# A new order of issue: gates' and down products in longer runs on TensorE

## The chip, the cores and the metric

One core of a Trainium2 chip runs the whole program. The metric is the device time of one execution in microseconds (us), and the time of a kernel is the median of several executions. Engines are named as in the profile: PE is TensorE (PEld its weight loads), DVE VectorE, ACT ScalarE, POOL GpSimd, and SP SyncE, which here only issues DMAs.

## The reference

An attention over 8 batches, 8 heads, 576 positions and 64 channels feeds a gated product chain over the 4608 tokens:

```python
q_d, k_d, v_d = (means of q, k, v over 4 positions)
out_up = repeat(softmax(q_d @ k_d.T / 8) @ v_d, 4)
mask = abs(pos[:, None] - pos[None, :]) < 4
out_local = softmax(where(mask, q @ k.T / 8, -1e9)) @ v
x = (out_up + out_local), as 4608 tokens x 512
a = x @ w1                      # 512 -> 1024
b = x @ w2
h = a * b @ w3                  # 1024 -> 1024
return h @ w_out                # 1024 -> 512
```

The inputs q, k, v and the four weights arrive as float32 or float64; the kernel takes the weights as 64-bit words where they are that.

## The kernel before, in words

**Stages.** First the product of `w3` and `w_out` is formed (`fold`, tasks `product m j`), so that `h @ w_out` becomes one product with 1024 rows and 512 columns, kept as a high and a low half in `wphl`. The weights come from HBM as 64-bit words in tiles `raw`, and DVE and ACT make float32 and then a high and a low part of each (`words`, `parted`, `gate_block`). Beside this runs the attention: `pooled` and `quad` for the part on means of four positions, and for the local part either `group_unit` with its scores and values on PE (the first two batches) or `unit` on DVE and ACT (the other six), where DVE multiplies and adds tiles of 128 x 768. Each unit ends in x, again a high and a low part, `xh` and `xl`.

**The chain of products.** The tokens go through `moe(c)` in 12 chunks of 384. For each chunk and each eighth `f` of the 1024 columns there are two gates' products, `which` 0 for `w1` and 1 for `w2`, into one PSUM tile `pab` each, 128 x 384. Each is two tasks of 6 matmuls. `three` (L317 to L319) issues the three matmuls of one product of high and low parts. Then ACT copies the first tile out (`copy_a`, L1062), DVE multiplies it with the second tile (L1064), ACT rounds the result to its high part `gh` (L1069) and DVE takes the low part `gl` (L1071). A down product of chunk c and eighth f is three tasks of three matmuls, `wphl` times `gh` and `gl`, summed over f in three PSUM tiles `acc`. There are two `pab` tiles (`BUFS["ab"]`), three `acc` tiles and three for everything else (`s_ps`, `t_ps`, `o_ps`, `se_ps`, `te_ps`, `oe_ps`). In the first gates' weights of a chunk (f 0 to 3) `w1a` belongs to the first tile and `w2a` to the second; for later f both are in `wo` or both in `wb`.

**What sets the order.** Nothing is scheduled on the chip. `Plan.add` collects 3208 tasks with their dependences and buffers (`Ring`). The table `ORDER` says, engine by engine, in which order that engine's tasks are issued; a number in it is the place of a task among its engine's tasks as `Plan.add` saw them, "78-86" a row of them. `Plan.order` merges the five lists, and each engine then runs its own list strictly in order, with waits where a task needs another's result or buffer:

```python
left[e] = [l[k] for w in ORDER[e].split() for a, _, b in [w.partition("-")]
           for k in range(int(a), int(b or a) + 1)][::-1]
```

A `pab` tile's next user is thus bound to its last reader by the ring of two:

```python
t, bank = add("PE", 6 * mm_us(CT), mmul, d, take=[R["ab"]], uses=[x_held[c]])
ta, ha = add("ACT", act_us(CT, psum=True), copy_a, [ends[0]], take=[R["a"]], uses=[banks[0]])
tg = add("DVE", dve_us(CT), ..., [ta, ends[1]], uses=[ha, banks[1]])
```

In the first 100 us SP's list also decides which load comes first: of the words of the weights (`raw`, L342), of `q` and `k` for `pooled_sums` (L688, L692) and of the values `v_w` for `group_unit` (L732).

Of the kernel before, what the change touches and what calls it, by code (L numbers as in the profile page):

```python
# [64 lines left out]
        "31-34 37 35-36 38-43 45 44 48 47 46 50-51 49 53 52 55-56 54 59 58 57 2 61 60 3 64 63 62 5 67 66 4 65 68-69 71-72 70 73 79 78 81 "  # L65
        "76 6 80 74-75 82 84 83 0 7 87 86 85 89 88 8 11 9-10 13 12 77 91-92 95 90 94 14-16 93 1 96-97 104 107 17 103 18-19 106 105 20 98 "
        "21-22 108-109 111 23 112 110 25-26 114 28 27 24 115 117 113 116 29 119 30 99-100 122 120 118 102 145 123 128 101 125 121 124 "
        "146 126 147 131 167 166 127 173 130 133 174-175 168 149 129 148 172 132 134 170-171 164-165 169 151 150 135-136 188 137 189-190 "
        "138 191 184 152 178 183 153 139-141 176 181 143 177 142 179 187 144 194 182 195 197 196 186 192 201 198 200 199 193 180 202-203 "
        "155 154 185 204 208 206 205 209 207 156 215 212 214 213 211 210 157 218 217 216 158 219-222 224 223 225 159 257 226 253 248 256 "  # L70
        "252 250 247 160 251 255 254 249 246 264 269 260 259 267 261 270 265 262 258 271 273 272 263 227 266 268 161-162 274 276 279 277 "
        "275 278 229 280 228 281 230-231 163 302-303 305 304 308 306 233 331 307 309 232 329 334 330 235 332-333 310 337-338 335-336 340 "
        "339 341 234 312-313 315 237 342 301 348 343 236 344-345 349 346 238 347 316-317 350 311 358 355 239 357 351 356 359 314 352 240 "
        "353 360 366 241 323 320 364 363 365 322 361-362 321 282 319 318 367 242 368-370 326 371-372 243 324 373 325 244 405 400 374 "
        "283-284 403 327 245 401-402 404 409 285 375-377 286 328 378 408 379 427 406 430 428 288 429 407 410 287 289 411 431-432 354 412 "
        "290 433-434 413 435-436 454 457 292 291 414 459 415 458 416 419 460 455-456 465 417 437 293-294 418 420 380 421 441 422 442 423 "
        "461-462 295-296 463 424 440 439 438 464 466 445 297 447-448 381 443 446 444 467-468 382 469-470 298 471 449 383 499 472 451 299 "
        "450 426 473 300 474-475 384 502 476 504 385 477 506 501 478 503 507 500 509 387 508 386 452 510 571 389 505 425 572-573 388 "
        "511-512 574 513 391 577 575 578 390 514-515 518-519 516 453 576 520 517 521-522 393 523 529 479 579 392 530 526-527 534 532 525 "
        "395 528 535 531 533 394 581 584 582 585 536 396 480 580 583 586 537 591 538-539 397 587 590 398 540 482 541-542 598 603 544 481 "  # L80
        "543 545 399 484 546-548 483 588 592 599 601 605 589 607 549 485 608-609 486 600 602 488 604 487 606 570 594 593 595 610 489 596 "
        "611-612 490 613 524 614 625 617-618 615-616 629 619 627 624 491 620 550 492 634 621 493 628 622 635 626 632 696 494-495 630 698 "
        "697 631 633 699 636 551-552 637 703 638 496 701 700 702 597 553 639-640 643 641-642 497 669 554-555 704 644-645 670 646 498 "
        "647-648 671-672 706 557 709 673-674 710 677 556 675 711 678 559 679-680 558 708 707 676 714 681 561 682 623 560 683-684 688 685 "
        "689 563 686-687 725 690 712 562 691 649 565 713 692-693 564 734 728 727 733 705 723 715 717 724 726 732 566 695 650 716 730-731 "
        "729 735 651-652 720 736-737 719 738 718 739 771 740 567 654 741 769 772 653 742 568 721 743 722 744 773 569 745 768 770 746 774 "
        "778 656 747 779 775 655 776 840-843 777 658 780 844 657 781-782 694 660 847 794 846 795 659 799 783 787 784 661 785-786 662 845 "
        "663 788-789 797 748 790-792 801 664 798 796 803 665 805 800 804 848 749 802 806 666 750 807-808 751 809-811 850 667-668 852 851 "
        "872 854 853 867 813 753 855 812 814-815 752 877 754 816 870 868 755 871 859 869 817 878 818 849 757 861 860 874 856 873 858 857 "
        "839 756 876 875 793 863 758 879 759 880-882 761 883 864 862 894 884 886-887 897 888 885 865 819 889 760 896 895 890-891 763 893 "  # L90
        "965 901 898 904 968 966 902 967 866 900 762 899 820 764 903 905 765 906 969 907 821 970 822 908-909 766 971-972 941 823 910 767 "
        "911 824 938 912 939 943 942 940 825-826 913-914 973 915-917 945 827 944 828 948 946-947 949 892 950 830 995 829 996 951 997 994 "
        "832 975 952 957 953 992 831 958 954-955 833 956 993 918 978 976 959-960 834 1002 835 980 919 961 1000 998 962 977 1003 979 985 "
        "999 920-921 1001 836 981 1004-1005 837 1006-1007 923 838 1008-1010 983 922 1037 1040 1039 925 1041-1042 1011-1013 924 974 986 "
        "1038 927 1014-1015 1043 1016 1045 926 1048 982 1044 984 963 929 1046 989 928 987-988 1047 930 964 1049 1064 931 990-991 1050 "
        "1068 1066 932 1067 1051 1017 1056-1057 933 1052 1063 1053 1058 1054-1055 934 1059 1074 1072-1073 1018 1065 1071 935 1069 "
        "1019-1020 1060 936 1061 937 1021-1022 1070 1075-1076 1023 1077-1078 1024 1079-1081 1026 1082-1085 1025 1086-1087 1028 1062 1027 "
        "1030 1029 1031 1088 1032-1033 1089 1034 1091 1035 1090 1092-1093 1036 1095 1094 1097 1096 1099 1098 1101 1100 1102-1106"
    ),
    DVE=(  # L100
        "1 0 55 2 56 3 57 59-61 4 58 62 5-7 63 8 11-12 9-10 64 13-14 66-67 15 65 69 22 68 71 73 70 74 23 72 76 32 31 75 33 78 80 77 81 "
        "79 16 83 82 85 87 34 84 86 35 88 38 36 90 37 89 91 17 96 98 94 99 97 92-93 100 40 18 101 39 103 102 41 19-20 105 104 24 42 106 "
        "43 46 45 44 108 107 110 112 25 30 109 21 26 111 27 113 119 181 121 95 120 114 123 28-29 47 124 48-49 122 182 130 183 125-126 50 "
        "128 131 51 127 52-53 129 54 115 173 116 133 180 132 137 135 174 157 117 138 175 136 176 134 159 158 139-140 142 118 144 187 184 "
        "145 141 146 191 143 161 188 177 160 192 178-179 194-195 163 162 185 147 196 189 148-149 197 190 193 150 186 151 201 152 154-155 "
# [1138 lines left out]
```

## Time and profile before

| what | value |
|---|---|
| median of 3 executions | 752.03 us (750.47 to 754.09) |
| the profiled execution, its own time | 751.62 us |
| its span, first to last instruction | 749.8 us |
| PE busy | 734.5 us, 98% of the span, 5378 matmuls |
| DVE busy | 612.3 us, 82% |
| ACT busy | 534.9 us, 71% |
| POOL busy | 110.9 us, 15% |
| mean granted clock of PE | 0.997 of full speed |

The profile is one execution. Busy time is what an engine's instructions covered; on PE matmuls overlap, and their ends are modelled, so the time from one start to the next tells more than the duration. In a timeline a row has the start in us from the span's begin, the duration in us, the engine, the line, the operation, what it writes and reads, and in brackets the idle time before it and what ended that.

### The profile page before, as it was taken

What the parts mean: (1) busy time and instruction counts of PE and PEld (TensorE: products, weight loads), DVE (VectorE), ACT (ScalarE), POOL (GpSimd) and SP (SyncE); (2) the same over time, 40 slices, a digit from 0 to 9 for tenths busy, and PEclk for the clock granted to TensorE, in tenths of its full rate; (3) what the DMA queues carried; (4) which work ended last, traced back from release to release, by engine and by line L of the source; (5) the groups of instructions that cost most, each with busy time, mean ns of one, the idle gap of its engine ahead of it and who ended that gap; (6) DMA issues with size and microseconds to landing.
All of it is one profiled execution on the core that took longest, in us unless ns stands there. A gap on an engine that the chain in (4) does not pass through costs nothing.

```text
span 749.8 us, 14982 instructions
## 1 busy us (share of the span) xinstructions
PE 734.5 (98%) x5378; PEld 661.8 (88%) x5378; DVE 612.3 (82%) x1028; ACT 534.9 (71%) x2101; POOL 110.9 (15%) x147
## 2 busy tenths in 40 slices
PE   7998999999999999999999999999999999999996
PEld 6776888888999989999989989899899999999995
DVE  5998996448999998999999999898999898865112
ACT  4897878567997976986886986787687795742211
POOL 4020003300212211122111211131120010010000
PEclk9999999999999999999999999999999999999999
DMA  9898855724786767498367764488555345322101
GB/s 306 268 278 253 270 163 110 139 56 143 176 219 153 167 154 208 97 209 218 66 168 195 155 160 128 109 206 208 141 95 151 98 95 149 83 46 41 43 1 42
DMA packets 49887, 111.91 MB, mean 149 GB/s; under 512 B 4996, under 2 KB 17284, under 8 KB 49812
## 3 DMA queue, kind: packets, MB, share of 16 engines
q0 software_dynamic: 14592, 38.94, 29.8%
q1 hardware_dynamic: 34932, 71.74, 28.8%
q8 instruction: 42, 0.69, 0.4%
q10 hardware_dynamic: 288, 0.27, 0.1%
q14 instruction: 33, 0.27, 0.1%
HBM read 80.26 MB, written 9.44 MB: 120 GB/s over the span
## 4 chain that ended last, share of the span: by engine, by line
PE 77%; DVE 11%; DMA 4%; ACT 4%; issue 2%; SPq 0%; DVEq 0%; ACTq 0%
PE pab L317 16%; PE pab L319 16%; PE pab L318 16%; PE acc L317 8%; PE acc L318 8%; PE acc L319 8%; DMA raw<-in_w_dram 3%; PE s_ps L614 2%; PE o_ps L575 1%; DVE wx L364 1%; PE t_ps L656 1%; ACT junk L911 1%; DMA xl<-pv 1%; DVE pr L901 1%; PE oe_ps L829 1%
## 5 line engine op out<-in xcount | busy, mean ns | idle before, releaser
L959 ACT ACTIVATE pv<-kv,s 128x64 f32<-128x64 f32 x432 | 116.9, 338 | 16.2 <-DVE s L936 14.7
L911 ACT ACTIVATE junk<-pr 128x64 f32<-128x64 f32 x432 | 110.3, 255 | 19.4 <-DVE pr L901 9.9
L901 DVE TENSOR_TENSOR pr<-q_t,kv 128x768 f32<-128x768 f32 x126 | 117.2, 950 | 1.5 <-DMA kv<-in_kw_dram 0.9
L317 PE MATMUL acc<-wphl,gh 128*128 128x512 f32 x288 | 114.4, 397 | 0.0
L319 PE MATMUL acc<-wphl,gl 128*128 128x512 f32 x288 | 113.4, 394 | 0.0
L318 PE MATMUL acc<-wphl,gh 128*128 128x512 f32 x288 | 113.3, 393 | 0.0
L975 POOL DMA_DIRECT2D xl<-pv x54 | 46.3, 857 | 364.0 <-DVE xl L977 299.5
L1064 DVE TENSOR_TENSOR a<-pab,a 128x384 f32<-128x384 f32 x96 | 52.9, 551 | 47.5 <-PE pab L319 35.5
L914 DVE TENSOR_REDUCE s<-pr 128x12 f32<-128x768 f32 x90 | 84.1, 946 | 0.3
L1062 ACT COPY a<-pab 128x384 f32<-128x384 f32 x96 | 45.2, 471 | 53.6 <-PE pab L319 45.8
L911 ACT ACTIVATION_READ_ACCUMULATOR junk<-pr 128x1 f32 x432 | 81.1, 188 | 0.0
L1069 ACT CAST gh<-a 128x384 fp32r<-128x384 f32 x96 | 48.6, 506 | 41.7 <-PE acc L318 22.5
L1071 DVE TENSOR_TENSOR gl<-a,gh 128x384 fp32r<-128x384 f32 x96 | 52.6, 548 | 22.7 <-ACT gh L1069 22.6
L967 DVE TENSOR_TENSOR pv<-kv,s 128x768 f32<-128x768 f32 x72 | 68.1, 950 | 0.2
L317 PE MATMUL pab<-xh,w1a 128*128 128x384 f32 x192 | 65.8, 343 | 0.5 <-ACT a L1062 0.4
L317 PE MATMUL pab<-xh,w2a 128*128 128x384 f32 x192 | 65.3, 340 | 0.3 <-DVE a L1064 0.3
L317 PE MATMUL pab<-xh,wo 128*128 128x384 f32 x192 | 65.4, 340 | 0.0
L317 PE MATMUL pab<-xh,wb 128*128 128x384 f32 x192 | 65.1, 339 | 0.0
L319 PE MATMUL pab<-xh,wb 128*128 128x384 f32 x192 | 64.6, 337 | 0.0
L319 PE MATMUL pab<-xh,w1a 128*128 128x384 f32 x192 | 64.5, 336 | 0.0
L319 PE MATMUL pab<-xh,w2a 128*128 128x384 f32 x192 | 64.5, 336 | 0.0
L319 PE MATMUL pab<-xh,wo 128*128 128x384 f32 x192 | 64.5, 336 | 0.0
(130 smaller groups left out, 1755.6 us busy)
## 6 DMA issues: line engine op xcount, KB each, us to landing
xl<-pv POOLq DMA_DIRECT2D x54, 384.0 KB, 4.0
raw<-in_w_dram SPq DMA_DIRECT2D x32, 512.0 KB
qks<-in_qk_dram POOLq DMA_DIRECT2D x18, 576.0 KB, 7.0
kv<-in_kw_dram SPq DMA_DIRECT2D x18, 576.0 KB
kv<-in_vw_dram SPq DMA_DIRECT2D x18, 576.0 KB
q_t<-in_q_dram SPq DMA_DIRECT2D x18, 384.0 KB
vs<-in_v_dram POOLq DMA_DIRECT2D x24, 256.0 KB, 5.5
out_dram<-o_sb SPq DMA_DIRECT2D x23, 256.0 KB
```

The source lines that it names most:

```text
L317: nc.tensor.matmul(out_ps, lhsT=lh, rhs=rh, start=first, stop=False)
L318: nc.tensor.matmul(out_ps, lhsT=lh, rhs=rl, start=False, stop=False)
L319: nc.tensor.matmul(out_ps, lhsT=ll, rhs=rh, start=False, stop=last)
L901: (nc.gpsimd if o in share["qk_pool"] else nc.vector).tensor_tensor(out=T[o], in0=T["q"], in1=T["k"][:, o * D:o * D + nq].rearrange("p (t ...
L911: nc.scalar.activation(out=junk, in_=T[o][:, t], func=AF.Copy, accum_out=T["s"][:, t, o:o + 1])
L914: reds.append(add("DVE", dve_us(nq), lambda o=o: nc.vector.tensor_reduce(out=T["s"][:, :, o], in_=T[o], op=ALU.add, axis=AX.X), [tp], uses ...
L959: nc.scalar.mul(out=T["pv", o][:, tt], in_=T["v"][:, (tt + o) * D:(tt + o + 1) * D], mul=T["s"][:, tt, o:o + 1])
L967: nc.vector.tensor_tensor(out=T["pv", o], in0=T["v"][:, o * D:o * D + nq].rearrange("p (t d) -> p t d", d=D), in1=T["s"][:, :, o].unsqueez ...
L975: t = add("Pool", 0.9, lambda o=o: nc.gpsimd.dma_start(out=T["x"], in_=T["pv", o], accum_op=ALU.add), [t, tm], uses=[hx, h], late=dma_us(1 ...
L1064: tg = add("DVE", dve_us(CT), lambda f=f: nc.vector.tensor_tensor(out=straight(T["a", f]), in0=turned(T["p", 1, f]), in1=straight(T["a", f ...
L1069: nc.scalar.copy(out=T["gh", f], in_=T["a", f])
L1071: tl = add("DVE", dve_us(CT), lambda f=f: nc.vector.tensor_tensor(out=T["gl", f], in0=T["a", f], in1=T["gh", f].bitcast(F32), op=ALU.subtr ...
```

## The change

All five lists of `ORDER` are replaced; the tasks, their dependences, buffers and instructions are the same, and five lines fewer hold the table, so that a line of the new kernel has a number smaller by 5 (L317 becomes L312). On PE, changes between a gates' and a down task that stand next to each other go from 321 to 106. A row of gates' tasks is mostly 1 to 3 long before, and mostly 3 to 9 now.

```diff
 ORDER = dict(
...
     PE=(
-        "13-14 16 0 17-18 1 15 21 19-20 23 2 25 27 24 29 22 26 28 30-33 37 34 36 35 39-40 38 41 3 44-45 42-43 4 46-47 49 51 48 50 52-53 "
+        "13-14 17 16 0 15 19-20 1 21 18 23 2 22 25-26 24 27-30 32-33 31 34 36-37 35 39 41 3 40 38 44 42-43 4 45-47 49 48 53 52 51 50 55 "
...
```

On PE, chunk 7: the second half of a gates' product into the first tile (`w1a`, f 2), and the next user of the second tile (`w2a`, f 2), whose last user (f 1) ended with the row ahead of this product. Before:

```order
L317 MATMUL pab<-xh_5883,w1a 128x384
L318 MATMUL pab<-xl_5884,w1a 128x384
L319 MATMUL pab<-xh_5883,w1a 128x384
L317 MATMUL acc_6269<-wphl,gh 128x512
L318 MATMUL acc_6269<-wphl,gh 128x512
L319 MATMUL acc_6269<-wphl,gl 128x512
L317 MATMUL pab<-xh_5883,w2a 128x384
```

In the changed kernel:

```order
L312 MATMUL pab<-xh_5907,w1a 128x384
L313 MATMUL pab<-xl_5908,w1a 128x384
L314 MATMUL pab<-xh_5907,w1a 128x384
L312 MATMUL pab<-xh_5907,w2a 128x384
L313 MATMUL pab<-xl_5908,w2a 128x384
L314 MATMUL pab<-xh_5907,w2a 128x384
```

The three matmuls of a down product between the two tiles have gone to another place: between the second tile's last use and its next use six matmuls of a gates' task stand now, where six and three stood before.

On SP, in the first 100 us: the loads of the values `v_w`, of `q` for the second batch's sums, and of weights (`raw`). Before:

```order
L732 DMA v_w<-in_v_dram 72x1x512
L688 DMA q_725<-in_qk_dram 128x4x288
L732 DMA v_w<-in_v_dram 72x1x512
L342 DMA raw<-in_w_dram 128x2x512
L732 DMA v_w<-in_v_dram 72x1x512
L342 DMA raw<-in_w_dram 128x2x512
L732 DMA v_w<-in_v_dram 72x1x512
```

In the changed kernel:

```order
L727 DMA v_w<-in_v_dram 72x1x512 x2
L337 DMA raw<-in_w_dram 128x2x512
L727 DMA v_w<-in_v_dram 72x1x512 x2
L337 DMA raw<-in_w_dram 128x2x512
L683 DMA q_799<-in_qk_dram 128x4x288
```

The load of `q` has moved from the second place to behind the four loads of `v_w` and two of weights.

## Rows read from the trace of the kernel before

**Rows 1.** Stretches: length, busy time and instructions by engine, clock, DMA share, GB/s
```profile
25.00:100.00 75.00, 72.28 (x697) 58.03 (x695) 70.56 (x135) 66.45 (x152) 5.20 (x6) 1.00 0.82 249
200.00:690.00 490.00, 489.42 (x3116) 448.88 (x3115) 445.37 (x698) 374.34 (x1632) 83.58 (x98) 1.00 0.62 145
690.00:750.00 60.00, 54.01 (x284) 49.97 (x282) 10.89 (x20) 10.75 (x22) 0.00 (x0) 0.99 0.09 27
```

**Rows 2.** Groups by line: count, then busy us, mean ns, and idle before
```profile
L317 PE MATMUL acc<-wphl,gh 128*128 128x512 f32 x288 | 114.4, 397 | 0.0
L317 PE MATMUL pab<-xh,w1a 128*128 128x384 f32 x192 | 65.8, 343 | 0.5 <-ACT a L1062 0.4
```

**Rows 3.** Timeline of PE, 500 to 510 us: start, duration, instruction
```profile
500.11 0.34 PE L317 MATMUL pab<-xh,w1a 128*128 128x384 f32 x1
...
503.23 0.39 PE L317 MATMUL acc<-wphl,gh 128*128 128x512 f32 x1
...
503.92 0.34 PE L317 MATMUL pab<-xh,wo 128*128 128x384 f32 x1
...
508.08 0.39 PE L317 MATMUL acc<-wphl,gh 128*128 128x512 f32 x1
...
509.45 0.34 PE L317 MATMUL pab<-xh,wo 128*128 128x384 f32 x1
```

**Rows 4.** Timeline of PE and ACT, 406 to 408 us, first tile
```profile
406.37 0.34 PE L319 MATMUL pab<-xh,wo 128*128 128x384 f32 x1
...
406.75 0.48 ACT L1062 COPY a<-pab 128x384 f32<-128x384 f32 x1 [1.28 <-PE pab L319]
...
407.59 0.35 PE L317 MATMUL pab<-xh,wb 128*128 128x384 f32 x1
```

**Rows 5.** Timeline of PE and DVE, 493 to 496 us, second tile
```profile
493.70 0.34 PE L319 MATMUL pab<-xh,w2a 128*128 128x384 f32 x1
...
494.43 0.55 DVE L1064 TENSOR_TENSOR a<-pab,a 128x384 f32<-128x384 f32 x1
...
494.90 0.94 DVE L914 TENSOR_REDUCE s<-pr 128x12 f32<-128x768 f32 x1
...
495.61 0.34 PE L317 MATMUL pab<-xh,w2a 128*128 128x384 f32 x1
```

**Rows 6.** Timeline around three late starts of gates' products
```profile
92.21 0.34 PE L319 MATMUL pab<-xh,w1a 128*128 128x384 f32 x1
...
92.89 0.44 PE L317 MATMUL pab<-xh,w2a 128*128 128x384 f32 x1 [0.34 <-DVE a L1064]
...
376.79 0.34 PE L319 MATMUL pab<-xh,w2a 128*128 128x384 f32 x1
376.87 0.27 ACT L929 ACTIVATE s<-s 128x84 f32<-128x84 f32 x1 [1.27 <-DVE gsm L637]
377.05 0.46 ACT L1062 COPY a<-pab 128x384 f32<-128x384 f32 x1
...
377.56 0.44 PE L317 MATMUL pab<-xh,w1a 128*128 128x384 f32 x1 [0.44 <-ACT a L1062]
...
434.19 0.34 PE L319 MATMUL pab<-xh,w2a 128*128 128x384 f32 x1
...
434.62 0.44 PE L317 MATMUL pab<-xh,w1a 128*128 128x384 f32 x1
```

**Rows 7.** Timeline of SP, DVE and PE, 57 to 71 us
```profile
58.21 0.98 SPq L732 DMA_DIRECT2D v_w<-in_v_dram  x1
59.25 0.42 SPq L688 DMA_DIRECT2D q<-in_qk_dram  x1
59.71 0.84 SPq L732 DMA_DIRECT2D v_w<-in_v_dram  x1
...
66.42 0.46 DVE L706 TENSOR_TENSOR qks<-q 128x288 f32<-128x288 f32 x1 [1.10 <-DMA q<-in_qk_dram]
...
70.19 1.32 PE L829 MATMUL oe_ps<-pte,v_w 72*32 72x64 f32 x80 [1.77 <-DMA v_w<-in_v_dram]
```

**Rows 8.** Timeline of PE, 11 to 16 us: the first product's third matmul
```profile
15.29 0.80 PE L319 MATMUL accw<-wo,w 128*128 128x512 f32 x1 [2.03 <-DVE w L381]
```

179 rows, old and new, of tables (ACT, DVE, PE, Pool) are left out of this document.

## The prediction, made before the changed kernel had run

> **What bounds the kernel now.** I read the page first, then the engines' busy time by stretches, then TensorE's instructions by group and in order of time, and beside them those of the engines that it waits for. The page gives PE the largest share; the stretches show where that matters: from 200 to 690 us PE is busy for 489.42 of 490 us, DVE for 445.37 (91%) and ACT for 374.34 (76%); after 690 us PE is almost alone; from 25 to 100 us PE, DVE and ACT are all near full [rows 1]. Since the ends of matmuls are modelled, what counts on PE is the distance from one start to the next. So PE is the bound, and DVE is close behind it. No reordering shortens PE's own work. A gates' matmul (2304 of them, 12 groups of 192) and a down matmul (864, 3 groups of 288) are busy 343 and 397 ns in the modelled form [rows 2], but start every 0.173 and 0.229 us: 24 gates' matmuls lie between 503.92 and 508.08 us (4.16 us), and 6 down matmuls between 508.08 and 509.45 (1.37 us) [rows 3]. That is about 399 + 198 us which both kernels hold. What a new order can change is what a change of kind costs, and the time PE waits.
>
> **What a change of kind costs: 0.5 us in all.** The same rows hold changes in both directions. From 500.11 to 503.23 us there are 18 gates' matmuls, the last followed by a down product: 3.12 us, again 0.173 each. From 503.23 to 503.92 there are 3 down matmuls, with a change before and one behind: 0.69 us, 0.230 each where the run of 6 had 0.228 [rows 3]. Three times 0.0017 us is 0.005 us for a pair of changes, so some 0.0025 us for one. 321 less 106 is 215 changes: 215 x 0.0025 = 0.5 us less. The bounds are 0 and, if the rows' rounding of 0.01 us hid a full step at each change, 2.2 us less.
>
> **What the longer runs cost: 2.9 us.** Gates' sums go into two PSUM tiles `pab`. The first of a pair is emptied by ACT (L1062), the second by DVE (L1064), and the next pair may begin only then. The quickest such turn: the last matmul into a tile starts at 406.37 us, ACT begins at 406.75 (0.38 later) and takes 0.48 [rows 4]; at 377.56 PE starts 0.05 us behind the copy's end [rows 6]. So a tile comes back 0.91 us after its last matmul's start. On DVE the operation takes 0.55 [rows 5], which makes it 0.98. Half a gates' product is 6 matmuls, 1.04 us; with 0.17 for the last matmul itself, a place with only half a product between last use and next use leaves 1.21 us, as at 406.37 to 407.59 [rows 4]. That fits by 0.30 us on ACT and 0.23 us on DVE, if the engine is free at once. Down products in between, three matmuls of 0.23 us each, give 0.69 us more. The place shown from the two orders is such a one: before, 1.91 us lie between 493.70 and 495.61, the reader on DVE starts 0.73 us after the last matmul and ends at 494.98, in time [rows 5]. In the new order the down product is gone, and with the same DVE the tile would come 0.12 us late (494.98 + 0.05 against 493.70 + 1.21).
>
> I counted these places in the two orders, as far as chunk 10 (in chunk 11 DVE and ACT are nearly idle: 10.89 and 10.75 us of the last 60 [rows 1]): 7 before, 27 now (16 wait for ACT, 11 for DVE). The 7 tell the price. Three of them delayed PE, taken as step less 0.173: 0.51 us at 92.89, 0.60 at 377.56, 0.26 at 434.62; four did not, the place at 407.59 among them [rows 4, 6]. At 377.05 the copy was late because ACT had waited for DVE for its earlier work [rows 6]. Of the five places behind 200 us that is 0.86 us, or 0.17 a place. Nineteen of the new 27 lie there, so 14 more: 14 x 0.17 = 2.4 us. Two new ones lie at about 90 us, where DVE and ACT are full: I add 0.5 us for them and nothing for the rest of the first two chunks. Bounds: 0, if the new order of DVE and ACT has each reader in time; and 14 x 0.72 = 10 us, if each reader stands behind a whole DVE operation of 0.94 us [rows 5] (0.94 + 0.98 - 1.21 = 0.71, rounded up).
>
> Here the Trainium skill has a rule against this change: its page Perfetto Trace Analysis, in the section on matmuls, says that independent groups of matmuls should rotate through different PSUM banks, so that ACT and DVE empty one while the next group runs. Runs of one kind rotate through two tiles where the mixed order used five. By the rule the sum would rise to its upper bound, 751.6 - 0.5 + 10 - 1.1 = 760 us; by the trace, with four of seven such places free, it is the sum below.
>
> **The first 100 us: 1.1 us less.** All five engines' orders are new, with small swaps. One has a visible effect. On SP's queue a load of q stood between the first and the second load of `v_w` (59.25 between the issues at 58.21 and 59.71 us); now all four `v_w` loads go ahead of it. At 70.19 PE had waited 1.77 us for `v_w`, and DVE had waited 1.10 us for that q at 66.42 [rows 7]. The q moves behind two weight loads as well, but its first reader on DVE now stands behind the first sum of `oe_ps`, which PE's products for it must precede. PE's wait goes; what is late next is DVE, which adds `oe_ps` and is near full in these 75 us [rows 1]. So I take DVE's 1.1 us, with 0 and 2 us as bounds. The first products wait for the decoded weights, the third matmul until 15.29 us with 2.03 us idle before it [rows 8]; DVE's order there is turned about, but up to the second turn of q it holds nearly the same operations, one low part of a weight in place of one sum of q. I take 0, from 1.5 less to 1.5 more. Behind it POOL's DMA adds are swapped in places; they wait for DVE and not DVE for them, so I cost them at nothing; if one came late, DVE's work on the next chunk would be late with it, which is the second rival.
>
> **Sum.** The profiled execution took 751.62 us (span 749.8 and 1.8 around it), 0.4 under the median of 752.03. 751.6 - 0.5 + 2.9 - 1.1 = 752.9; I say 753.0 us. A measurement of this kernel can tell about 0.5% (3.8 us) from no change, so this is none.
>
> **The rivals.**
> *The tiles come back late.* One mechanism, at the 20 new places: the reader on DVE or ACT is held by the operation in front of it. Held for half an operation, 0.47 us, DVE's tile is 0.47 + 0.98 - 1.21 = 0.24 us late; held for a whole one, 0.71. For it: DVE's 91%, and the place of [rows 5]. Against it: four of seven such places cost nothing, and the readers' places on DVE and ACT were reordered too. Midway, 20 x 0.45 = 9 us in place of 2.9: 759 us. It decides beyond the 0.5% from about 0.25 us a place.
> *DVE becomes the bound.* Of 490 us DVE has 45 idle. If longer runs make it wait longer for a product and later work waits for it, some 10% more idle is 4.5 us, given to PE whenever a chunk's x is not ready: 757 us. Against it: DVE's sum of work is unchanged.
> *The first 100 us tighten.* If the 2 us at `v_w`, 1.5 us at the first products and half a microsecond at later places all go, and the tight places cost nothing: 751.6 - 0.5 - 4 = 747 us.
> *A change costs what rounding hides.* 2.2 us in place of 0.5: 751.2 us, still no change.
>
> **How the numbers follow.** My forecast with the last rival has 0.62, late tiles 0.22, DVE as the bound 0.06, a tighter start 0.10. So faster 0.10, same 0.62, slower 0.28. The range runs from 748.4 (2 us gone at `v_w`, half of the 1.5 us at the first products, tight places free: 751.6 - 0.5 - 2 - 0.7) to 759.0 (the first rival's midpoint); some 2 in 10 lie outside.
>
> **What would show it.** Starts of matmuls at a change of kind should stay at 0.17 and 0.23 us. The waits of PE and its weight loads for `a` on ACT and DVE should grow from some 1.4 us to 3 to 5. The wait of `oe_ps` for `v_w` should be gone. Wrong would be: a change that costs 0.02 us or more, PE's waits for `a` over 7 us, or a third matmul of the first product that starts more than 2 us away from 15.29 us.

## The result, and the profile after

The new order took 760.81 us (median of 5 runs, 758.31 to 770.75) beside 753.6 for the kernel before (5 runs, 750.47 to 754.87): a ratio of 1.0104, interval 1.0062 to 1.0145; the ratio leaves out the run of 770.75 us, a slow one with a granted clock of 0.990. The new order is slower by 1.0%, and its time lies above the range given. The profiled execution took 760.81, with a span of 758.8 us, 9.0 longer than before's 749.8.

Where the 9 us went is seen when the span is cut in stretches. The columns are those of [rows 1]: length, busy us and instructions of PE, PE's weight loads, DVE, ACT and POOL, granted clock, DMA share, GB/s. First the new kernel up to 690 us:

```profile
0.00:100.00 100.00, 93.15 (x861) 74.56 (x865) 89.53 (x172) 80.21 (x176) 13.41 (x33) 1.00 0.84 264
100.00:200.00 100.00, 98.88 (x1131) 87.84 (x1124) 68.05 (x139) 69.78 (x273) 15.47 (x18) 1.00 0.53 133
200.00:300.00 100.00, 93.56 (x643) 83.28 (x643) 85.43 (x137) 77.33 (x348) 17.17 (x20) 0.98 0.68 158
300.00:690.00 390.00, 389.23 (x2424) 357.20 (x2423) 354.84 (x556) 294.74 (x1279) 64.95 (x76) 1.00 0.59 139
```

And the same four stretches of the kernel before:

```profile
0.00:100.00 100.00, 91.12 (x875) 73.97 (x875) 87.62 (x171) 79.67 (x173) 13.39 (x33) 0.98 0.83 260
100.00:200.00 100.00, 100.00 (x1111) 88.98 (x1108) 68.44 (x141) 70.14 (x276) 13.98 (x18) 1.00 0.53 135
200.00:300.00 100.00, 99.96 (x694) 91.07 (x693) 93.95 (x154) 82.73 (x369) 20.26 (x24) 1.00 0.77 180
300.00:690.00 390.00, 389.46 (x2423) 357.81 (x2422) 351.42 (x545) 291.61 (x1264) 63.32 (x74) 1.00 0.58 136
```

From 200 to 300 us PE stands still for 6.4 us and does 51 matmuls fewer; DVE and ACT are less busy too (85.43 for 93.95, 77.33 for 82.73), so nobody there has become the bound by work. From 300 to 690 us the two kernels are alike to 0.23 us. **PE's loss** is here what is left over when every matmul's distance to the next start is taken less 0.173 us (gates') or 0.227 us (down and the first product's); of the short matmuls of the attention only distances over 0.4 us count, less 0.1. From 200 to 300 us it is 11.0 us where it was 2.1. That is 8.9 us. The first 100 us lose 1.3 us less than before, the second 100 us 1.1 more, all behind 300 us 8.7 in both.

What PE waited for from 200 to 300 us in the new kernel (waits: engine, its tile and line, the releaser; us in total, times, longest). Before, this view has no row for PE as the waiting engine:

```profile
PE t_ps L651 <- ACT pexp L640: 3.4, 2, 2.4
PE pab L312 <- DVE a L1059: 2.3, 1, 2.3
PE pab L312 <- ACT a L1057: 0.6, 1, 0.6
```

These waits are 6.3 of the 8.9 us. Another 1.7 us are the matmuls right behind the wait of 2.3 us, which start every 0.32 us in place of 0.173 while the granted clock is down (the last section has the rows). From 300 us to the end, the new kernel:

```profile
PE s_ps L609 <- ACT oup L583: 0.4, 1, 0.4
PE pab L312 <- DVE a L1059: 0.2, 1, 0.2
```

So the places where a `pab` tile comes back late cost 0.2 us behind 300 us. Of the 6.3 us of waits from 200 to 300 us, 5.7 come from three additions into the pooled tile `xl`. Each unit's `xl` begins as one product and takes six more, `pv`; three of these six additions are made by an accumulating DMA that POOL issues (L970), and DVE's next addition (L972) waits until that DMA has landed. The second such DMA of unit 7, in the timeline of POOL, DVE, ACT and PE of the new kernel:

```profile
235.69 0.84 POOL L970 DMA_DIRECT2D xl<-pv  x1 [5.21 <-DVE xl L972]
...
240.83 0.24 DVE L921 TENSOR_REDUCE mx<-s 128x12 f32<-128x84 f32 x1
243.41 0.96 DVE L972 TENSOR_TENSOR xl<-xl,pv 128x768 f32<-128x768 f32 x1 [2.33 <-DMA xl<-pv]
244.28 0.24 DVE L923 TENSOR_TENSOR s<-s,mx 128x84 f32<-128x84 f32 x1
244.44 0.16 DVE L631 TENSOR_SCALAR gsm<-gsm 128x4 f32<-128x4 f32 x1
...
244.62 0.28 ACT L924 ACTIVATE s<-s 128x84 f32<-128x84 f32 x1 [2.76 <-DVE gsm L631]
245.30 0.71 ACT L640 ACTIVATE pexp<-pexp,gsm 128x144 f32<-128x144 f32 x2 [0.40 <-DVE gsm L632]
...
246.84 1.06 PE L651 MATMUL t_ps<-ident,pexp 128*128 128x128 f32 x6 [0.99 <-ACT pexp L640]
```

It is read from the bottom: PE waits for ACT's `pexp`, ACT for DVE's small operations on `gsm`, and these stand on DVE behind an addition that waits 2.33 us for the DMA. The DMA issued at 235.69 landed 7.7 us later; DVE had 5.4 us of other work for it. Before, the same pair:

```profile
230.76 0.89 POOL L975 DMA_DIRECT2D xl<-pv  x1 [1.85 <-DVE xl L977]
...
238.63 0.19 DVE L647 TENSOR_TENSOR pexp<-pexp,gsm 128x32 f32<-128x32 f32 x1
238.73 0.25 DVE L933 TENSOR_REDUCE sm<-s 128x12 f32<-128x96 f32 x1
238.89 0.95 DVE L977 TENSOR_TENSOR xl<-xl,pv 128x768 f32<-128x768 f32 x1
```

There 8.1 us lay between issue and addition, the DMA took 6.0, and the operations for `pexp` stood ahead of the addition. The second place is unit 6's first DMA, issued at 198.18 and landed at 205.54, in the timelines of DVE and PE:

```profile
205.63 0.96 DVE L972 TENSOR_TENSOR xl<-xl,pv 128x768 f32<-128x768 f32 x1 [3.34 <-ACT junk L906]
...
209.31 0.54 PE L312 MATMUL pab<-xh,w2a 128*128 128x384 f32 x1 [2.33 <-DVE a L1059]
```

The row of the addition names an ACT instruction, but the addition follows the landing by 0.09 us, and in the run below in which one entry of POOL's list moves, where the landing comes at 203.19, it starts at 203.28. The third place is unit 8's second DMA, which had this to landing, by the view of the tile from 268 to 276 us:

```profile
DMA to landing us min/median/max: 8.7/8.7/8.7
```

Over the whole run the same line reads 3.9/4.2/9.7 us, before 3.9/4.0/8.3; 11 of the 54 took over 6 us, before 4. At the three places both the landing and the cover (the time that DVE's other work fills behind the issue) got worse, at units 6 and 8 the landing more, at unit 7 the cover:

| unit and DMA | landing before, after | cover before, after | DVE waits after |
|---|---|---|---|
| 6, first | 4.5, 7.4 us | 5.3, 4.1 us | 3.3 us |
| 7, second | 6.0, 7.7 us | 8.1, 5.4 us | 2.3 us |
| 8, second | 5.8, 8.7 us | 6.4, 5.4 us | 3.3 us |

Unit 8's landing held ACT as well as DVE, in the timeline of the two:

```profile
277.66 0.96 DVE L972 TENSOR_TENSOR xl<-xl,pv 128x768 f32<-128x768 f32 x1 [3.27 <-DMA xl<-pv]
277.71 0.59 ACT L954 ACTIVATE pv<-kv,s 128x64 f32<-128x64 f32 x2 [3.77 <-issue]
278.20 0.69 ACT L640 ACTIVATE pexp<-pexp,gsm 128x128 f32<-128x128 f32 x2
```

ACT's wait has no releaser in the profile ("issue"), but it ends with the landing at 277.63: a new `pv` takes one of three buffers, and the DMA reads the oldest until it lands. Behind it stands `pexp`, and PE's wait of 2.4 us for that.

A second thing changed places. In the new order the first loads of `vs` and `vl` of batch 2 stand on SP behind four loads of `v_w`, at 142.09 us; before they were issued at 133.42. POOL's accumulating loads for that batch so run until 167 us and not 153, beside two more `v_w` loads (SP, 156.29 and 157.77), and PE waits, in the timeline of POOL and PE:

```profile
162.34 0.78 POOL L533 DMA_DIRECT2D vl<-in_v_dram  x1 [0.68 <-DMA vl<-in_v_dram]
164.32 1.32 PE L824 MATMUL oe_ps<-pte,v_w 72*32 72x64 f32 x80 [1.12 <-DMA v_w<-in_v_dram]
```

### The profile page after: what moved, and what is told of

It reads as the page before. It is cut to its first block, busy times and chain, and to the rows that moved or that the text cites. A ratio compares the mean times of both kernels' runs of the same rounds, so it can differ in the third digit from the quotient of the medians.

```text
span 758.8 us, 14971 instructions
## 1 busy us (share of the span) xinstructions
PE 738.2 (97%) x5378; PEld 661.6 (87%) x5378; DVE 614.0 (81%) x1028; ACT 535.1 (71%) x2101; POOL 111.0 (15%) x147
## 4 chain that ended last, share of the span: by engine, by line
PE 58%; DVE 17%; DMA 15%; ACT 5%; issue 4%; SPq 0%; POOL 0%; DVEq 0%; ACTq 0%; POOLq 0%
PE pab L312 12%; PE pab L314 11%; PE pab L313 11%; PE acc L312 6%; PE acc L313 6%; PE acc L314 6%; DMA xl<-pv 4%; DVE pr L896 3%; DMA raw<-in_w_dram 3%; DVE s L909 3%; DMA qks<-in_qk_dram 3%; DMA raw<-in_wout_dram 2%; DVE pv L962 2%; DVE xl L972 2%; DMA v_w<-in_v_dram 1%
## 5 line engine op out<-in xcount | busy, mean ns | idle before, releaser
L312 PE MATMUL acc<-wphl,gh 128*128 128x512 f32 x288 | 114.5, 398 | 0.0
L970 POOL DMA_DIRECT2D xl<-pv x54 | 46.9, 868 | 337.6 <-DVE xl L972 283.8
L312 PE MATMUL pab<-xh,w2a 128*128 128x384 f32 x192 | 65.8, 343 | 2.6 <-DVE a L1059 2.5
L312 PE MATMUL pab<-xh,wb 128*128 128x384 f32 x192 | 65.6, 342 | 0.6 <-ACT a L1057 0.6
L312 PE MATMUL pab<-xh,w1a 128*128 128x384 f32 x192 | 65.9, 343 | 0.2
L312 PE MATMUL pab<-xh,wo 128*128 128x384 f32 x192 | 65.4, 341 | 0.0
L1066 DVE TENSOR_TENSOR gl<-a,gh 128x384 fp32r<-128x384 f32 x96 | 52.6, 551 | 15.3 <-ACT gh L1064 15.3
L972 DVE TENSOR_TENSOR xl<-xl,pv 128x768 f32<-128x768 f32 x54 | 51.3, 949 | 16.9 <-DMA xl<-pv 12.1
L313 PE MATMUL pab<-xl,w1a 128*128 128x384 f32 x192 | 64.9, 338 | 0.0
L313 PE MATMUL pab<-xl,w2a 128*128 128x384 f32 x192 | 64.7, 337 | 0.0
```

The lines of the kernel that those rows point to most:

```text
L312: nc.tensor.matmul(out_ps, lhsT=lh, rhs=rh, start=first, stop=False)
L313: nc.tensor.matmul(out_ps, lhsT=lh, rhs=rl, start=False, stop=False)
L972: t = add("DVE", dve_us(nq), lambda o=o: nc.vector.tensor_tensor(out=T["x"], in0=T["x"], in1=T["pv", o], op=ALU.add), [t, tm], uses=[hx, h])
L1066: tl = add("DVE", dve_us(CT), lambda f=f: nc.vector.tensor_tensor(out=T["gl", f], in0=T["a", f], in1=T["gh", f].bitcast(F32), op=ALU.subtr ...
```

## The experiments

All 18 runs use either the old or the new order of issue with one edit. Numbers in the lists are tasks of one engine's program. Each time is a median, beside the kernel before on the same chip.

### From where on the new order loses

Two hybrids first: the new order up to 195 us and the old one behind (in each of the five lists, the tasks issued by then stand as in the new order and the rest as in the old; 302 changes of kind), and the old order up to 300 us and the new one behind.

> The new order up to the task that PE begins at 195 us, the old order for all that is left; 302 changes of kind. Theory 1 (late adds): the 9 us came between 200 and 300 us, where three accumulating DMAs of pv into xl land late and hold DVE; with the old order there, the time is that of the old kernel, 751 to 754 us. Theory 2 (the start): the new order's first 195 us leave DVE and PE in a worse state, and the loss comes whatever follows: 758 to 761 us.

Measured 757.3 us beside 753.19, ratio 1.0061, 1.0022 to 1.0099: between the two expectations. So part of the loss can come ahead of 195 us; the runs spread from 753.37 to 760.21. The one profiled was the fastest; in it PE waits 1.30 us for `v_w` at 163.60, as in the new order.

> The old order up to the task that PE begins at 300 us, the new order for the rest; 162 changes of kind, so the long runs stand in the last 450 us. Theory 1 (late adds between 200 and 300 us): 751 to 755 us. Theory 3 (long runs cost as such, some 0.25 us at each place where half a product separates two uses of a tile): 16 such places before chunk 11 lie behind 300 us, 4 us more than the old kernel, 756 to 759 us. If a change of kind cost 0.02 us, this kernel would be 3 us faster than the old one.

Measured 753.46 beside 753.19, 1.0015, 0.9999 to 1.0030. Over 400 us of long runs, with 162 changes in place of 321, neither gain nor lose. Then the reverse of the first (old up to 195 us, new behind, 125 changes):

> The old order up to the task that PE begins at 195 us, the new one for the rest; 125 changes of kind. Theory 1 (late adds between 200 and 300 us): the new order of that stretch is in it, so 757 to 761 us. If the loss needs the new order of the first 195 us as well (the first of the late adds meets a transfer that is issued at 188 to 197 us), 753 to 755 us.

Measured 762.05 beside 753.56, 1.0093, 1.0068 to 1.0117: what stands behind 195 us is enough for the whole loss, and by the run before most of it lies ahead of 300. But not every execution keeps to that. The one profiled here, the slowest at 767.3 us, loses 15.3 us behind 300 us in place of 8.7, most of it where DVE waits for SP's load of `q_t`, in the timeline of DVE and PE:

```profile
529.68 0.96 DVE L895 TENSOR_TENSOR pr<-q_t,kv 128x768 f32<-128x768 f32 x1 [4.98 <-DMA q_t<-in_q_dram]
...
531.16 0.69 PE L311 MATMUL pab<-xh,wb 128*128 128x384 f32 x1 [3.41 <-DVE a L1058]
```

No run tests that place alone.

### With the accumulating DMAs of q, k and v left out

```diff
-                lq = add("Pool", 0.9, lambda f=f: nc.gpsimd.dma_start(out=raws[b][0], in_=qk4[b, f], accum_op=ALU.add), ...
+                lq = add("Pool", 0.9, lambda: None, ...
```

and the same for `v`, in the new order and in the old:

> The new order, with the accumulating DMAs that sum q, k and v over four positions left out for batches 2 to 7 (that part of the computation is missing: 18 of 576 KB, and the v's). Theory 1: with that company gone the adds of pv land in about 4 us, DVE's idle time on them falls from 15 us to under 6, and 6 to 9 us of the span go, 750 to 754 us. Theory 3: the same 758 to 761 us, less what the old order gains by the same cut.

> The old order with the same accumulating DMAs left out. Theory 1: the old kernel hardly waits for late adds (3 us of DVE's idle time), so it gains at most 2 us, 750 to 753 us, and the two orders lie within 3 us of each other. Theory 3: the difference of 7 to 8 us between the two orders stays.

Measured 753.42 (1.0001, 0.9981 to 1.0022) and 752.64 (0.9994, 0.9976 to 1.0013), both beside 753.19. The two orders differ by 0.8 us without these transfers and by 7.2 with them. Changes of kind and long runs are the same with and without, so they alone are not the cause; most of the loss needs these transfers in the queues. Not all of it does: unit 7's second addition still landed after 7.8 us, where 4 were expected, beside four loads of SP (issued from 230.28 to 231.60, the DMA at 231.88), and PE's loss from 200 to 300 us is 5.3 us, in the old order without them 3.1.

### Single entries of POOL's list moved

```diff
     Pool=(
-        "... 30 33 21-23 36 ... 35 37 51 38 28-29 ..."
+        "... 30 21 33 22-23 36 ... 35 37-38 28 51 29 ..."
```

33 and 51 are accumulating loads of `qks`; 21 and 28 are additions of units 6 and 8. Both moved, one moved, and the mirror image (33 ahead of 21) in the old order:

> The new order with two entries of POOL's list moved and nothing else: the second accumulating DMA of q and k for the fourth batch goes behind unit 6's first add of pv, and the second one for the fifth batch behind unit 8's second add of pv. Theory 1: two of the three late adds land in 4 to 6 us, DVE's 3.3 us of idle time at each shrinks to under 1.5, and 4 to 6 us of the 9 are back: 754 to 757 us. If collisions on POOL's queue do not matter: 758 to 761 us.

> The new order with the first of these two moves alone. Theory 1: the add of pv issued at 198 us lands in 4 to 5 us in place of 7.4, PE's wait of 2.3 us for the product at 209 us goes, 2 to 3 us less than the new order: 757 to 759 us.

> The old order with the mirror of that move: the accumulating DMA of q and k is put ahead of unit 6's first add of pv, as in the new order. Theory 1: that add lands 2 to 3 us later, DVE has 0.8 us of slack there and waits 1 to 2 us, of which PE loses 0 to 2 us: 752 to 755 us. If this one swap were the whole cause, 757 us or more.

Measured 761.16 (1.0084, 1.0047 to 1.0122), 761.02 (1.0090, 1.0063 to 1.0117) and 754.02 (1.0000, 0.9984 to 1.0016) beside 753.56. The two repairs gained no time: the first addition of unit 6 did land sooner (5.1 and 5.2 us for 7.4), but unit 7's still took 7.8 and 8.0, and unit 8's 6.3 with both moved and 9.4 with one. With both moved PE's loss from 200 to 300 us did fall, to 4.8 us. What took it back lies elsewhere, most of it ahead: from 100 to 200 us the loss is 8.6 us where the new order had 5.1, with a wait of 2.16 us for `v_w` at 166.5 us and a granted clock of 0.61 from 165 to 170 us.

```profile
100.00:200.00 100.00, 97.56 (x1116) 85.29 (x1114) 63.47 (x135) 66.41 (x259) 13.68 (x16) 0.97 0.52 130
200.00:300.00 100.00, 97.86 (x677) 87.79 (x677) 91.46 (x143) 81.54 (x369) 18.91 (x22) 1.00 0.71 162
```

The mirror image made unit 6's landing 6.3 us long in place of 4.5; DVE waited 1.04 us for it, and the time stayed, within the 752 to 755 expected.

### What stands behind the wait, moved ahead of it

On DVE the three additions go behind 2.7 to 3.6 us of other work (with unit 8's goes one product `pv`):

```diff
     DVE=(
-        "... 234 309 323 311 235 236 ... 374 340 375 393 376 394 377-378 402 395 267 ... 419 385 345 422 447 449 ..."
+        "... 234 323 311 235 236 309 ... 374-375 393 376 394 377-378 402 395 267 340 ... 419 345 447 449 385 422 ..."
```

> The new order; only VectorE's list changes. Three of its additions into a pooled tile (xl<-xl,pv), each of which waits for an accumulating DMA, now stand behind 2.7 to 3.6 us of other VectorE work that stood behind them: unit 6's (205.63 us in the profile after), unit 7's (243.41) and unit 8's (277.66). DMAs, POOL, SP, PE and ACT keep their lists. Theory A (VectorE's queue is in order, and the new order left these additions 4.1 to 5.4 us after their DMA's issue where landing takes 7.4 to 8.7): VectorE's idle time before the three, 3.3 + 2.3 + 3.3 us, falls below 2 us in sum, PE's loss from 200 to 300 us falls from 11 us to 3 to 5, and the time is 753 to 757. Theory B (the transfers' company itself costs, whoever waits; a wait cured here comes back at the next tile): 759 to 762 as with the new order.

Measured 760.89 beside 753.01, 1.0125, 1.0086 to 1.0165: Theory B, although the additions do what A asks: none of the three waits now. The same landings stop others: at 204.45 DVE waits 2.87 us to make the next `pv` (no buffer is free), and ACT 4.4 us at unit 8's. PE's loss from 200 to 300 us is 12.3 us. With the load of `vs` and `vl` moved too:

```diff
     SP=(
-        "... 68 77 69-71 78 72 ..."
+        "... 68 77-78 69-72 ..."
```

> As the kernel with the three later additions, and on SP the first loads of vs and vl of pooled 2 stand ahead of group_unit 4's second v_w load, as in the old order, and not four loads behind. Theory A: POOL's accumulating loads of that batch, which in the new order run from 147 to 167 us beside two v_w loads, end before 160 us; PE's wait for v_w at 163 us (1.1 us in the profile after, 2.2 in that of the two POOL entries moved) goes, and with it some 2 us of matmuls at a lower clock behind it where that came; 752 to 755.5, and 0.5 to 2 us under the kernel with the three later additions. Rival: the loads only change places and something else comes late: no difference to that kernel.

Measured 760.96, 1.0099, 1.0068 to 1.0130: no difference, as the rival said. And, without that load's move, with two of ACT's multiplications behind `pexp`:

```diff
     ACT=(
-        "... 448 467 446 444 468 ..."
+        "... 448 446 444 467-468 ..."
```

> The new order with VectorE's three additions later, and on ACT two multiplications of unit 9 into pv (277.71 us in the profile after), which take a buffer that an accumulating DMA holds until it lands, behind the last two divisions of pexp of that batch's quad 3 1. Transfers as they were. Theory 2 (what stands behind the wait costs): PE's wait for t_ps at 273 to 276 us (2.6 us after, 3.2 with VectorE's change alone) goes, and the time is 756 to 759, 2 to 4 us under the 760.9 with VectorE's change alone. Theory 1: the wait comes back at the next user of the ring, 759 to 762.

Measured 765.59 beside 752.26, 1.0178, 1.0150 to 1.0206, worse than all others and above both expectations. PE's loss from 200 to 300 us is 11.8 us; a further 3.3 us more than in the new order fall between 100 and 200 us, at `v_w`. The wait came back at the next taker of a buffer, and this time with a down product's eviction behind it on ACT, in the timeline of ACT and PE:

```profile
287.97 0.59 ACT L953 ACTIVATE pv<-kv,s 128x64 f32<-128x64 f32 x2 [3.90 <-DMA xl<-pv]
...
289.08 0.79 PE L311 MATMUL acc<-wphl,gh 128*128 128x512 f32 x1 [3.02 <-ACT o_sb L1081]
```

In these three runs, moving what waits cured nothing: the late landing stopped whoever came next.

### The mirror image, and the load of q, in the old order

Unit 7's second addition forward past 4.8 us of DVE's work, and in another kernel the load of `q` (57) behind two more loads of `v_w` and two of weights (not quite as in the new order, where the last of the four `v_w` loads, 7, stands ahead of it too):

```diff
     DVE=(
-        "... 314 265 370 266 372 393 ... 376 340 402 ..."
+        "... 314 265 340 370 266 372 393 ... 376 402 ..."
...
     SP=(
-        "... 27-36 4 57 5 37 6 38 7 39-40 ..."
+        "... 27-36 4-5 37 6 38 57 7 39-40 ..."
```

> The mirror image in the old order: only VectorE's list changes, and only unit 7's second addition behind a DMA (238.89 us in the profile before) is moved forward, past 4.8 us of other VectorE work, so that 3.3 us lie between its DMA's issue and it and landing takes 6.0. Theory A: VectorE idles 2 to 3 us there, PE waits for a (one of the moved instructions is the gates' product's second step) for 1 to 2.5 us, and the time rises by 1 to 3 us: 754 to 756.5 beside 753.5. Theory B: no change, 753 to 754, since the transfers are those of the old order.

> The old order; only SP's list changes: the q load of pooled_sums 1, which stood ahead of two v_w loads, stands behind them, as in the new order. By the prediction's term for the first 100 us, PE's wait of 1.77 us for v_w goes and the time falls by about 1.1 us, to 752.4 beside 753.5 (ratio 0.9985); by the rival, what waits for q takes it back and the ratio is 1.000.

The first measured 755.27 beside 753.01, 1.0027, 1.0012 to 1.0042, in the middle of Theory A's 754 to 756.5. Its timeline has the two waits that the new order has at 205 and 209 us:

```profile
239.16 0.96 DVE L977 TENSOR_TENSOR xl<-xl,pv 128x768 f32<-128x768 f32 x1 [2.30 <-DMA xl<-pv]
...
241.50 0.44 PE L317 MATMUL pab<-xh,wo 128*128 128x384 f32 x1 [1.97 <-DVE a L1064]
```

So one addition that stands too early costs some 2 us in an order that is otherwise the old one. The second measured 755.88, 1.0033, 1.0019 to 1.0048: slower, where 0.9985 was expected. PE's wait for `v_w` went, and a longer one came, since DVE's list still had the sums of `q` in front of the decoded weights:

```profile
71.30 0.46 DVE L706 TENSOR_TENSOR qks<-q 128x288 f32<-128x288 f32 x1 [5.87 <-DMA q<-in_qk_dram]
...
74.21 0.80 PE L319 MATMUL accw<-wo,w 128*128 128x512 f32 x1 [3.19 <-DVE w L381]
```

### The landings themselves taken away

Three of the 54 accumulating DMAs made by DVE, where POOL issued them:

```diff
+ON_DVE = {(6, 2), (7, 4), (8, 4)}
...
-                    t = add("Pool", 0.9, lambda o=o: nc.gpsimd.dma_start(out=T["x"], in_=T["pv", o], accum_op=ALU.add), ...
+                    t = add("Pool", 0.9, lambda o=o, i=i: nc.vector.tensor_tensor(out=T["x"], in0=T["x"], in1=T["pv", o], op=ALU.add) if (n, i) in ON_DVE else nc.gpsimd.dma_start(out=T["x"], in_=T["pv", o], accum_op=ALU.add), ...
```

> The new order, and three of the 54 accumulating DMAs xl<-pv are made by VectorE instead, at the place where POOL issued them: unit 6's first, unit 7's second, unit 8's second, the three that landed 7.4 to 8.7 us after their issue. VectorE has 3 x 0.95 us more work there, and nothing waits for those landings. Theory 1 (the landing time costs, whoever waits): VectorE's 8.9 us of idle time at the three and ACT's 3.8 us before pv at 277.71 go, PE's loss from 200 to 300 us falls from 11 us to 4 to 6, time 754 to 757. Theory 3 (the transfers' company costs in other ways): 759 to 762.

> As the kernel with three additions on VectorE, with three more (the second of units 15, 17 and 21, which landed after 8.2 to 9.7 us) and, on SP, the first loads of vs and vl of pooled 2 ahead of group_unit 4's second v_w load as in the old order. Theory 1: 752.5 to 756, some 1 to 1.5 us under the kernel with three, from the wait for v_w at 163 us (1.1 us) and little from the three later ones, which cost PE nothing in the profile after. Theory 3: as the kernel with three.

With three: 757.58 beside 752.26, 1.0078, 1.0062 to 1.0093. PE's loss from 200 to 300 us fell from 11.0 to 3.9, by a little more than Theory 1 said (4 to 6), but the time lies just above its 754 to 757. The other wait is left, and larger in this profile: from 100 to 200 us the loss is 8.2 us, 3.1 more than in the new order (and 1.3 more behind 300 us). PE's waits for `v_w`, and the stretches around them:

```profile
164.00 0.32 PE L825 MATMUL oe_ps<-pte,v_w 72*32 72x64 f32 x8 [0.96 <-DMA v_w<-in_v_dram]
165.59 1.59 PE L825 MATMUL oe_ps<-pte,v_w 72*32 72x64 f32 x80 [1.27 <-DMA v_w<-in_v_dram]
```

```profile
160.00:165.00 5.00, 3.37 (x35) 2.79 (x33) 1.49 (x3) 2.91 (x7) 1.63 (x2) 1.00 0.92 206
165.00:170.00 5.00, 4.41 (x87) 3.67 (x88) 2.87 (x7) 1.43 (x3) 0.00 (x0) 0.66 0.46 89
```

With six, and `vs` and `vl` loaded earlier: 752.12, 1.0002, 0.9986 to 1.0018 (12 runs). The loss is gone, by a little more than the 752.5 to 756 expected.

Without the accumulating loads of batches 3 and 4 alone:

```diff
-                lq = add("Pool", 0.9, lambda f=f: nc.gpsimd.dma_start(...
+                lq = add("Pool", 0.9, (lambda: None) if b in (3, 4) else lambda f=f: nc.gpsimd.dma_start(...
```

> The new order, with the accumulating DMAs of the pooling of q, k and v left out for batches 3 and 4 alone (the k, q and v sums of these two batches are then the first term only); all additions xl<-pv stay. Theory 3 (their company makes the additions late in this stretch): landings of the three additions fall to 4 to 6 us, PE's loss from 200 to 300 us to 4 to 6 us, time 753 to 757, near the 753.4 without the transfers of all six batches. If company elsewhere matters: 757 to 760.

Measured 757.78 beside 752.26, 1.0093, 1.0072 to 1.0114, just above the 753 to 757 of Theory 3. Within the stretch it is half right: PE's loss from 200 to 300 us is 4.6 us, and the additions of units 6 and 8 land after 5.0 and 4.8 us, but unit 7's after 7.8, as without all six batches. What is left to the 753.4 without all six is 0.7 us of waiting for `v_w` at 165 us, which needs batch 2's transfers, and behind 300 us a loss of 11.2 us where the run without all six has 8.1; which transfers cost that is not shown.

Which of the two cures of the kernel with six did it? The last two runs complete the square:

> The new order with the three additions on VectorE (757.6 alone) and the first loads of vs and vl of pooled 2 one place ahead of group_unit 4's second v_w load. If the load is what the kernel with six had over that with three: 752 to 753.5. If the three more additions are: 756.5 to 758.

> The new order with that load alone moved. If the two cures add up: the new order's 760.8 less what the load gives with the additions cured (up to 5 us), 755.5 to 757.5. If the late landings take it back, as in the kernel with VectorE's additions later and the load (761.0): 759 to 761.

| | `vs`, `vl` as in the new order | `vs`, `vl` loaded earlier |
|---|---|---|
| additions as in the new order | 760.81 (1.0104, 1.0062 to 1.0145) | 761.28 (1.0107, 1.0067 to 1.0147) |
| three additions on DVE | 757.58 (1.0078, 1.0062 to 1.0093) | 753.98 (1.0014, 0.9990 to 1.0038) |

The four cells were measured beside medians of 753.6, 753.31, 752.26 and 753.31 us for the kernel before, so the ratios are to be compared and not the times. The two cures do not add up. The load alone gives nothing, and with the additions cured 0.64% (4.8 us). The additions alone give 0.26% (2.0 us), which the intervals do not tell from nothing, and with the load 0.93% (7.0 us). The three further additions of the kernel with six give at most 0.12%, and the intervals overlap; 753.98 lies just above the 752 to 753.5 expected if the load did it, and far from the 756.5 to 758 expected if these additions did. In the kernel with both cures the third stretch reads:

```profile
200.00:300.00 100.00, 98.63 (x683) 88.71 (x682) 94.85 (x157) 80.94 (x361) 17.18 (x20) 1.00 0.68 162
```

683 matmuls for 643 after and 694 before: most of the loss is back. Why the load alone gives nothing stays open. Its profile shows no wait for `v_w` at 164 us, the three late additions still there (DVE idle 1.5, 2.1 and 3.2 us), and DVE waiting 3.18 us for the load of `q_t` at 525 us, with 0.94 us of it passed on to PE. But that is its fastest run of six (758.65 to 766.19), and one profile does not show what the slower ones lost.

No version of the new order that does all the work was faster than the kernel before: the best has a ratio of 1.0002.

## Why the prediction was wrong

**The step that failed** is the sentence on POOL's DMA adds: "they wait for DVE and not DVE for them, so I cost them at nothing". The words "not DVE for them" are wrong. DVE's next addition waits for each landing, and so does, through the three buffers, the maker of a later `pv`. From 200 to 300 us the new order's profile has 8.9 us more of PE's loss than before, and with three of these additions made by DVE it is 3.9 us in place of 11.0. In time the term was worth 0.93% (7.0 us) with `vs` and `vl` loaded earlier; without that it was 0.26%, which is not clear of the noise. For the rest a second step failed with it: of the small swaps on all five engines it says "One has a visible effect". SP's list behind 100 us was not priced, and there the later loads of `vs` and `vl` made PE wait for `v_w` at 164 us; with the additions cured, moving them back gives 0.64%.

The prediction's own condition, "if one came late", was the right question. The trace of before held part of the answer: landings of 4.5, 6.0 and 5.8 us could be compared with the cover that is left in the new order, 4.1, 5.4 and 5.4 us. That would have shown three additions 0.4 to 0.6 us late, and a term that is not nothing, but not its size: the landings themselves grew to 7.4, 7.7 and 8.7 us, since other transfers stand around them.

**DVE as the bound**, the second rival (757 us, 0.06), has the right engine and the wrong mechanism. It let DVE wait longer for products. DVE waits for transfers, and PE for operations that stand behind; DVE's work did not grow (614.0 us for 612.3).

**Changes of kind, -0.5 us:** right, they are nearly free. The kernel with six additions on DVE has the new order's 106 changes on PE and takes what the old one takes; the one with the new order behind 300 us has half the changes and gains nothing. In the new kernel the first down matmul behind a gates' one still takes 0.230 us to the next, as in [rows 3].

**Longer runs, +2.9 us:** over-sized. Of the 27 places with 1.21 us, 20 have 0.2 to 0.37 us to spare; apart from the one at 209.31 those that delayed PE sum to 0.6 us, 0.02 us a place where 0.17 was taken from five old places [rows 6]. Those five were not a sample of tight places; they were late because DVE or ACT was. PE's waits for `a` are 3.1 us in all, within the 3 to 5 foretold, yet 2.3 of it is the one at 209.31 behind a late landing. (That place is itself one of the 27: by an estimate from [rows 3], three down matmuls in it would have left 0.7 us less of the wait.) The 1.4 us foretold as their value before is the sum of the three late starts; by the view of waits PE and its weight loads waited 4.7 us before, 0.7 and 4.0, and 10.5 after, 3.1 and 7.4. The prediction put 760 us to the rule of the Trainium skill (Perfetto Trace Analysis, the section on matmuls), and 760.81 came; still the trace does not bear that price out, since the waits for an emptied tile behind 300 us are 0.2 us. A right total can come by a wrong way, and here that is luck.

**The first 100 us, -1.1 us:** right in size (1.3 us less), by luck, and wrong in its source. The run with the load of `q` moved nearly as far, and nothing else, is slower by 0.33%. What the profile shows the new order to have gained is the third matmul of the first product, which starts 1.83 us earlier than in [rows 8]:

```profile
13.46 0.50 PE L314 MATMUL accw<-wo,w 128*128 128x512 f32 x1 [0.20 <-DVE w L376]
```

The prediction had that at 0, with 1.5 us to either side. The wait of `oe_ps` for `v_w` of [rows 7], said to be gone, is now 0.35 and 0.33 us at 76 us, and a new one of 1.12 us stands at 164.32.

## What to carry to other kernels

When an order of issue changes, list every wait on a transfer, not only those on engines: for each, the work that lies on the waiting queue between issue and wait in the new order, against the landing time that the old trace shows in company, then what the new order issues just ahead of the transfer, and also who takes the transfer's buffer next. Here late landings were cured at the transfer (another engine made it); moving the instruction that waits only passed the wait on. With two losses side by side a cure of one may not show in the time, so its own stretch of the profile has to be read too. And a gain that a reordering aims at should be priced first: here what it aimed at, changes of kind, had nothing to give.

## What the runs showed of the hardware

An accumulating DMA of 384 KB from SBUF into SBUF landed 3.9 us after its issue where nothing else moved (issued at 229.62 us in the new kernel). With other transfers in flight it took 7.4 us (unit 6's, 1.5 us behind an accumulating load of 576 KB), 7.7 (unit 7's, behind four loads of SP) and 8.7 (unit 8's, behind transfers of POOL and of SP); the eleven over 6 us took 6.6 to 9.7. Putting that load of 576 KB ahead of unit 6's in the old order took its landing from 4.5 to 6.3 us. Before, four took over 6 us and none shows in PE's waits; in the new order three of eleven make most of the loss.

A stall of PE can cost more than itself, since the granted clock can fall behind it. After the 2.33 us at 209.31, where ten gates' matmuls from 209.65 on start every 0.32 us in place of 0.173, the new kernel's stretches read

```profile
205.00:210.00 5.00, 2.67 (x15) 2.33 (x14) 4.37 (x6) 3.65 (x20) 0.85 (x1) 0.95 0.37 69
210.00:215.00 5.00, 5.00 (x23) 5.00 (x22) 4.44 (x6) 1.65 (x9) 0.27 (x1) 0.71 0.82 256
```

and after the 3.02 us at 289.08 the kernel with DVE's and ACT's instructions moved has

```profile
285.00:290.00 5.00, 1.43 (x3) 1.02 (x4) 4.52 (x7) 2.03 (x7) 1.73 (x2) 0.81 1.07 201
290.00:295.00 5.00, 5.00 (x17) 4.80 (x16) 0.33 (x1) 4.89 (x21) 0.00 (x0) 0.50 0.68 160
```

with 17 matmuls in 5 us: 0.50 of 2.4 GHz is the lower level, 1.2 GHz. But the wait of 2.41 us before 278.64 in the new kernel has no such fall in its stretch or the next:

```profile
275.00:280.00 5.00, 2.59 (x18) 2.13 (x17) 2.34 (x4) 1.66 (x6) 0.85 (x1) 1.00 0.57 171
280.00:285.00 5.00, 5.00 (x27) 4.53 (x26) 5.00 (x6) 4.66 (x19) 0.00 (x0) 1.00 0.82 193
```

So a stall of this length may or may not take the clock with it; that executions of one kernel differ by this is likely, but no run here separates it.
